# Retention and a gated feed-forward on one core: the first batch cast and transposed by pairs of heads, every second score tile in other banks

## The chip, the cores and the metric

The kernel runs on one core of a Trainium2 chip. A core has five engines that each work through their own queue in order: TensorE (PE, with PEld for its weight loads), VectorE (DVE), ScalarE (ACT), GpSimd (POOL) and SyncE (SP), which here only issues DMAs. ACT's queue issues DMAs too, the transposing ones. The metric is the time of one execution on the device, in microseconds; less is better.

## The reference

`B, H, S, D` are 8, 8, 576 and 64; the feed-forward goes from 512 to 2048 and back, over 4608 tokens.

```python
scores = scale * np.matmul(q, k.transpose(0, 1, 3, 2))
Dmat = np.where(rel >= 0, gamma[:, None, None] ** rel[None, :, :], 0.0)
attn = np.matmul(scores * Dmat[None], v)
x = attn.transpose(0, 2, 1, 3).reshape(B * S, H * D)
h = x @ w_in
out = (h * np.clip(h + 3.0, 0.0, 6.0) / 6.0) @ w_out
```

So each head's scores decay with distance and are causal; there is no softmax. The heads' outputs side by side are the rows of x, and those go through two matrix products with a hard swish between them.

## The kernel before

**Tiling.** Each batch has 576 positions: four chunks of 128, and a tail of 64. Two batches' tails are packed into one chunk, so there are 36 chunks. The decay is split into a factor on Q and factors on K and V, which the casts to fp16 multiply in; what is left of it within a chunk is a 0/1 mask (`mask01`, or `maskt` for a tail). Across chunks a running state, K transposed times V, carries the past.

**Steps.** The order of all work is written out in a string, `PROGRAM` (L35 to L79), and `act` (L628) carries out its words one after the other. Since each engine's queue is in order, the string sets for each engine what comes behind what. The words:

- `L i.h` (load0) loads half of the heads of Q (i = 0) or K (i = 1) of batch 0; `V t` loads a chunk of V of batch 0; `l n` (load) loads Q, K and V of chunk n; `W a.i` (wload) loads block i of w_in (a = 0) or w_out (a = 1), 512 KB each. All of these are issued on SP, in this order.
- `C` (cast0, L203) casts the first batch's Q or K by halves of the heads, `c n.i` (cast, L161) casts chunk n's Q, K or V, `w a.i` (wcast, L547) casts a weight block. The last letter is the engine: v for VectorE, g for GpSimd, s for ScalarE.
- `X` (xpose0, L218) transposes the first batch's Q or K on PE and copies it from PSUM to `wout16`, which stands in as its place until w_out is cast into it. `K` (kback, L232) transposes K back, for the state. `y n` (xpose_pe, L254) transposes chunk n on PE with a copy from PSUM; `x n` (xpose, L176) does it by a transposing DMA on ACT's queue.
- `s n` (ret1, L269) computes chunk n's scores into PSUM and masks them on DVE into `at` (L284); a number after it says how many warm matmuls, which compute nothing that is used, go ahead.
- `o n` (ret2, L292) multiplies the masked scores by V and adds what the state gives (L300, L306), updates the state (L325), copies the result on ACT to `xt` (L330) and casts the state on ACT to `s16` (L336), which the next chunk's `o` reads.
- `u` (up, L365) and `h` (up_half, L371) are pieces of the first product of the feed-forward: matmuls (L369, L385), a relu on ACT (L352), and on DVE the rest of the hard swish (L357).
- `p j` is a piece of the second product for batch 0, in the plain way (L412), with copies to `osb` after p7. For the other batches the second product is made of seven smaller ones, `P b.j` (product, L454), with sums of blocks built on DVE by `e b.j` (enc, L429) and `t j` (tbuild, L561).

**Banks.** PSUM has a tile "sc" of two banks (scores), "xp" and "st" of one each, and four buffers "mm" of one bank each, which X, K, h, u, p and P take in turn. The next user of a buffer waits until the one before has been read.

Of the kernel before, what the change touches and what calls it, by code (L numbers as in the profile page):

```python
# [10 lines left out]
FP32 = mybir.dt.float32  # L11
FP16 = mybir.dt.float16
ACTF = mybir.ActivationFunctionType
ALU = mybir.AluOpType
# [18 lines left out]


PROGRAM = """  # L35
H19 L0.0 L0.1 L1.0 L1.1 C0.0v C0.1v V0 W0.0 W0.1 V1 V2 V3 W0.2 W0.3 c0.2g
C1.0v X0.0s W0.7 X0.1s X1.0s C1.1v X1.1s s0.4 K0v w0.0s s1 c1.2g K1v o0
w0.1g s2.8 o1 s3 c2.2g w0.2g o2 h0.0.0.1 W0.4 c3.2g o3 W0.5 h0.0.2.3 w0.3v
W1.0 h0.1.0.1.8 W1.6 W0.6 W1.7 W1.1 W1.2 w0.5g h0.1.2.3 W1.3 l4 l5 W1.4 W1.5
u0.4 u0.5 u0.6 l6 w0.7g u0.7 w0.4g u0.8 w1.7s u0.9 l7 w0.6g w1.3g w1.6v  # L40
c4.0g u0.10 w1.0s u0.11 u0.12 u0.13 u0.14 u0.15 w1.1g c4.1v c5.0g p0 y4v l8
w1.2s p1 s4 p2 c5.1g y5v p3 w1.5s l9 c4.2g s5 w1.4g o4 t0 c5.2g p4 l10 l11
c6.0g c6.1g c6.2v c7.0v c7.1v c7.2g l12 c8.0g p5 y6s p6 l13 t1 c8.1g o5 s6
c9.0g c9.1g c8.2g p7 y7v h1.0.0.8 h1.0.1.9 s7 o6 h1.0.2.10 h1.0.3.11 l14
c9.2g l15 c10.0g c10.1g c11.0g c11.1g c10.2g x8 h1.0.4.12 h1.0.5.13 o7 x9
h1.0.6.14 h1.0.7.15 h1.1.0.8 h1.1.1.9 h1.1.2.10 h1.1.3.11 e1.1.0.4 h1.1.4.12
t2 h1.1.5.13 c11.2g l16 x10 l17 c12.0g c12.1g h1.1.6.14 c12.2g h1.1.7.15
e1.1.4.8 e1.2.0.8 s8 t3 P1.0 x11 P1.1 e1.3.0.8 P1.2 o8 c13.0g c13.1g c13.2g
s9 P1.3 x12 e1.4.0.8 P1.4 l18 o9 l19 c14.0g c14.1g c14.2g P1.5 P1.6 h2.0.0.8
h2.0.1.9 s10 x13 h2.0.2.10 h2.0.3.11 h2.0.4.12 o10 l20 s11 x14 c15.0g  # L50
h2.0.5.13 h2.0.6.14 o11 s12 c15.1g c15.2v h2.0.7.15 h2.1.0.8 h2.1.1.9 l21
s13 o12 h2.1.2.10 h2.1.3.11 x15 h2.1.4.12 c16.0g c16.1g c17.0g e2.1.0.4
c17.1g c16.2g l22 c17.2g h2.1.5.13 h2.1.6.14 x16 h2.1.7.15 o13 c18.0g
e2.1.4.8 e2.2.0.8 x17 P2.0 s14 c18.1g P2.1 e2.3.0.8 l23 P2.2 s15 o14 c19.0v
c19.1g c18.2g e2.4.0.8 x18 P2.3 s16 o15 l24 P2.4 x19 c19.2g P2.5 s17 o16
c20.2g P2.6 l25 u3.0 u3.8 s18 o17 u3.1 c20.0g c20.1g c21.0g c21.1g c21.2g
u3.9 x20 u3.2 u3.10 u3.3 l26 c22.2g c22.0g c22.1g u3.11 e3.3.0.4 u3.4 x21
e3.1.0.4 l27 u3.12 u3.5 u3.13 o18 c23.0g c23.1g s19 u3.6 u3.14 c23.2g u3.7
u3.15 e3.1.4.8 e3.2.0.8 P3.0 s20 o19 l28 c24.0g e3.4.0.8 P3.1 x22 P3.2
e3.3.4.8 c24.2g P3.3 s21 o20 x23 P3.4 c25.2g P3.5 c24.1g c25.0v c25.1g s22  # L60
P3.6 l29 l30 u4.0 u4.8 o21 u4.1 u4.9 c26.0g u4.2 x24 l31 c26.1g c26.2v l32
u4.10 u4.3 o22 c27.0g u4.11 u4.4 u4.12 e4.3.0.4 u4.5 u4.13 e4.1.0.4 x25 s23
u4.6 c27.1g c27.2g u4.14 u4.7 u4.15 e4.1.4.8 e4.2.0.8 l33 s24 o23 e4.3.4.8
c28.0g c28.1g x26 P4.0 c28.2g P4.1 P4.2 s25 e4.4.0.8 l34 o24 c29.0g c29.1g
c29.2g P4.3 x27 x28 l35 P4.4 P4.5 s26 o25 P4.6 u5.0 u5.8 u5.1 u5.9 s27 o26
u5.2 u5.10 u5.3 u5.11 e5.3.0.4 e5.1.0.4 x29 c30.2g c30.0g c30.1v u5.4 u5.12
u5.5 u5.13 s28 o27 u5.6 u5.14 u5.7 u5.15 x30 e5.1.4.8 e5.2.0.8 c31.2g c31.0g
c31.1g c32.2g c32.0g e5.4.0.8 P5.0 P5.1 c32.1g s29 o28 x31 c33.0g x32 c33.1v
P5.2 e5.3.4.8 P5.3 s30 o29 x33 P5.4 P5.5 P5.6 u6.0 u6.8 u6.1 c33.2v s31 u6.9
u6.2 o30 u6.10 u6.3 s32 o31 u6.11 u6.4 c34.0g c34.1g c35.0g x34 e6.1.0.4  # L70
u6.12 u6.5 o32 s33 u6.13 e6.3.0.4 u6.6 u6.14 u6.7 u6.15 e6.1.4.8 e6.2.0.8
s34 c35.1g c34.2g o33 e6.3.4.8 x35 P6.0 e6.4.0.8 P6.1 P6.2 P6.3 s35 o34
c35.2v P6.4 P6.5 o35 P6.6 u8.0 u8.8 u8.1 u8.9 u8.2 u8.10 u8.3 u8.11 u8.4
u8.12 u8.5 u8.13 u8.6 e8.1.0.4 u8.14 u8.7 u8.15 e8.1.4.8 e8.2.0.8 e8.3.0.4
P8.0 P8.1 e8.4.0.8 P8.2 P8.3 e8.3.4.8 P8.4 P8.5 P8.6 u7.0 u7.8 u7.1 u7.9
u7.2 u7.10 u7.3 u7.11 e7.1.0.4 u7.4 u7.12 u7.5 e7.3.0.4 u7.13 u7.6 u7.14
u7.7 u7.15 e7.1.4.8 e7.2.0.8 e7.3.4.8 e7.4.0.8 P7.0 P7.1 P7.2 P7.3 P7.4 P7.5
P7.6
"""  # L79
E_TAIL = 544  # L80

# [2 lines left out]
def kernel(  # L84
# [9 lines left out]
    nc = tc.nc  # L94
    B, H, S, D = q.shape
    NTOK, DM = out.shape
    DFF = moe_w_in.shape[1]
    P = 128
    HP = H // 2
# [87 lines left out]
    qk0 = {}  # L187
# [12 lines left out]
            qk0["st"][:, ix, hs, :, :].rearrange("p h r d -> p h (r d)"),  # L200
            src.rearrange("h (p r) d -> p h (r d)", r=4))

    def cast0(ix, hh, eng):  # L203
        hs = slice(4 * hh, 4 * hh + 4)
        tab = (tq if ix == 0 else tkv)[:, 5:9, hs].rearrange("p r h -> p h r")
        out = (qk0["16"][:, ix, :, :].rearrange("p r (h d) -> p h r d", h=H)
               [:, hs, :, :])
        eng.tensor_tensor(out=out, in0=qk0["st"][:, ix, hs, :, :],
                          in1=tab.unsqueeze(3).to_broadcast([P, 4, 4, D]),
                          op=ALU.mult)  # L210

    def copy(eng, dst, src):
        if eng == "v":
            nc.vector.tensor_copy(dst, src)
        else:
            nc.scalar.copy(dst, src)

    def xpose0(ix, hh, eng):  # L218
        tp = psum.tile([P, 2, 4, P], FP16, tag="mm", bufs=4, name="tp")
        for a in range(2):  # L220
            for r in range(4):
                n0 = (2 * hh + a) * P
                nc.tensor.transpose(tp[:, a, r, :],
                                    qk0["16"][:, ix, r, n0:n0 + P], ident)
        p0 = 4 * ix + 2 * hh
        dst = wout16[:, p0:p0 + 2, :].rearrange("z a (p r) -> z a p r", r=4)
        copy(eng, dst, tp.rearrange("z a r p -> z a p r"))
        if ix == 1 and hh == 1:
            for t in range(NC4):
                qkTs[(0, 0, t)] = wout16[:, 0:8, t * P:(t + 1) * P]  # L230

# [18 lines left out]
    def warm(ps, n, w=P):  # L250
        for _ in range(n):
            nc.tensor.matmul(ps, zero16[:, 0:P], zero16[:, 0:w], start=True, stop=True)
# [13 lines left out]
        else:  # L266
            nc.scalar.copy(qt, tp)

    def ret1(c, nwarm=0):  # L269
        kind, b, t = c  # L270
        qt = qkTs[c]
        sc = psum.tile([P, 2, HP, P], FP32, tag="sc", name="sc")
        if nwarm:
            warm(sc[:, 0, 0, :], nwarm)
        for p in range(HP):
            for z in range(2):
                nc.tensor.matmul(sc[:, z, p, :],  # L277
                                 qt[z * D:z * D + D, HP + p, :],
                                 qt[z * D:z * D + D, p, :],
                                 start=True, stop=True)  # L280
        at = work.tile([P, 2, HP, P], FP16, tag="at", bufs=2, name="at")
        ats[c] = at
        m = mask01 if kind == 0 else maskt
        nc.vector.tensor_tensor(  # L284
            out=at.rearrange("p z a i -> p (z a) i"),
            in0=sc.rearrange("p z a i -> p (z a) i"),
            in1=m[:, :].unsqueeze(1).to_broadcast([P, 2 * HP, P]),
            op=ALU.mult)

    state = [None]  # L290

# [284 lines left out]
    order = []  # L576
# [51 lines left out]
    def act(w):  # L628
        kind, n, e = w[0], [int(x) for x in w[1:].rstrip("svg").split(".")], w[-1]
        if kind == "H":  # L630
            xp = psum.tile([P, HP, P], FP32, tag="xp", name="xp")
            warm(xp.rearrange("p a n -> p (a n)"), n[0], BLK)
        elif kind == "L":
            load0(*n)
        elif kind == "C":
            cast0(*n, ENG[e])
        elif kind == "X":
            xpose0(*n, e)
        elif kind == "K":
# [66 lines left out]
```

## Time and profile before

| | |
|---|---|
| median of 5 runs | 305.73 us (304.67 to 307.56) |
| profiled execution | 304.67 us, of which the span of the engines' work is 302.5 us |
| PE | 290.5 us busy, 2887 matmuls |
| DVE, ACT, POOL | 237.6, 141.3, 109.5 us busy |
| DMA | 53.93 MB, 178 GB/s over the span |
| PE granted clock | full throughout |

A group's line in the profile has the source line, the engine, the operation, what it writes and reads, a count, and then the busy time. In an answer by time the first two numbers are start and duration in us, from the span's start; several neighbours of one kind are merged (x4), and what ended the engine's idle time before stands in brackets. A list of waits has engine and line, what ended the wait, the total in us, how often, and the longest. A busy PE is not PE at its peak: matmuls are pipelined and their ends modelled.

### The profile page before, as it was taken

How to read it: one execution, taken by the hardware profiler on the slowest of the kernel's cores; microseconds unless marked ns; L12 is line 12 of the kernel's file. 1: busy time of each engine (PE TensorE's matmuls, PEld its weight loads, DVE VectorE, ACT ScalarE, POOL GpSimd, SP SyncE). 2: the span in 40 equal slices, each digit the busy share in tenths (PEclk: the TensorE clock that was granted, in tenths of full speed). 3: DMA queues.
4: the chain of work that ended last, by engine and by line, in shares of the span. 5: the costliest groups of instructions: out<-in, count | busy, mean ns of one | idle time of the engine just before them, and what ended most of it. 6: DMA issues, size and time to landing. Idle time of an engine off the chain costs nothing.

```text
span 302.5 us, 7125 instructions
## 1 busy us (share of the span) xinstructions
PE 290.5 (96%) x2887; PEld 198.4 (66%) x2887; DVE 237.6 (79%) x335; ACT 141.3 (47%) x259; POOL 109.5 (36%) x120
## 2 busy tenths in 40 slices
PE   8669999998999999999999999999999999999995
PEld 2456445787788878547854786468556864684584
DVE  6567858779959898799778967998699767957963
ACT  2656804764237633574156425743386226405610
POOL 3164374868455535657176153334300000000000
PEclk9999999999999999999999999999999999999999
DMA  7999999999999999999999999999312130014004
GB/s 239 300 293 394 288 279 217 218 201 200 297 148 195 239 220 226 213 197 220 221 212 199 265 211 191 213 218 201 122 38 19 52 106 0 0 46 96 2 0 139
DMA packets 149728, 53.93 MB, mean 178 GB/s; under 512 B 134848, under 2 KB 145088, under 8 KB 149696
## 3 DMA queue, kind: packets, MB, share of 16 engines
q1 hardware_dynamic: 120128, 46.15, 71.0%
q10 hardware_dynamic: 29568, 7.34, 17.9%
q8 instruction: 22, 0.36, 0.6%
q14 instruction: 10, 0.08, 0.1%
HBM read 36.70 MB, written 9.44 MB: 153 GB/s over the span
## 4 chain that ended last, share of the span: by engine, by line
PE 88%; SPq 4%; DVE 3%; DMA 2%; POOL 1%; ACT 0%; issue 0%
PE ph L369 31%; PE accB L483 10%; PE ph L385 9%; PE accC L483 9%; PE accA L483 9%; PE accD L483 5%; PE po L412 5%; PE xp L300 4%; PE sc L277 3%; DMA wst<-in_moe_w_in_dram 2%; SPq L247 2%; PE xp L306 2%; SPq L539 1%; DVE g L357 1%; PE state L325 1%; DVE ss L447 1%
## 5 line engine op out<-in xcount | busy, mean ns | idle before, releaser
L357 DVE SCALAR_TENSOR_TENSOR g<-u,ph 128x512 f16<-128x512 f32 x144 | 95.6, 684 | 25.4 <-ACT u L352 24.2
L352 ACT ACTIVATE u<-ph 128x512 f32<-128x512 f32 x144 | 84.2, 597 | 66.1 <-PE ph L369 38.0
L369 PE MATMUL ph<-xt,win 128*128 128x512 f16 x368 | 82.5, 379 | 0.0
L369 PEld LDWEIGHTS <-win 128*128 128x128 f16 x432 | 41.4, 98 | 47.7 <-issue 0.3
L483 PEld LDWEIGHTS <-ss 128*128 128x128 f16 x512 | 48.8, 98 | 8.6 <-DVE ss L447 2.4
L172 POOL TENSOR_TENSOR v<-st,tkv 128x512 f16<-128x512 f32 x31 | 35.4, 1145 | 47.8 <-DMA st<-in_v_dram 32.8
L284 DVE TENSOR_TENSOR at<-sc,mask 128x1024 f16<-128x1024 f32 x32 | 39.0, 1219 | 7.7 <-PE sc L277 7.6
L172 POOL TENSOR_TENSOR qk<-st,tq 128x512 f16<-128x512 f32 x29 | 31.4, 1083 | 35.2 <-PE state L325 14.5
L483 PEld LDWEIGHTS <-g 128*128 128x128 f16 x384 | 36.9, 98 | 5.5
L172 POOL TENSOR_TENSOR qk<-st,tkv 128x512 f16<-128x512 f32 x28 | 32.4, 1159 | 8.4 <-DMA st<-in_k_dram 4.1
L385 PE MATMUL ph<-xt,win 128*128 128x256 f16 x288 | 33.3, 273 | 0.0
L330 ACT ACTIVATE xt<-xp 128x512 f16<-128x512 f32 x32 | 19.1, 597 | 28.1 <-PE xp L306 20.9
L483 PE MATMUL accB<-tmat,ss 128*128 128x256 f16 x256 | 30.7, 273 | 0.3 <-DVE ss L447 0.2
L483 PE MATMUL accA<-wout,g 128*128 128x256 f16 x256 | 30.6, 273 | 0.0
L385 PEld LDWEIGHTS <-win 128*128 128x128 f16 x288 | 27.4, 98 | 3.6
L447 DVE TENSOR_TENSOR ss<-g 128x1024 f16<-128x1024 f16 (+1 forms) x30 | 21.9, 732 | 0.3
L300 PE MATMUL xp<-at,v 128*64 128x128 f16 x288 | 19.9, 225 | 1.5 <-POOL v L172 1.5
L300 PEld LDWEIGHTS <-v 128*64 128x64 f16 x288 | 14.0, 109 | 8.1 <-issue 2.5
L336 ACT CAST s<-state 64x256 f16<-64x256 f32 x48 | 17.3, 361 | 0.5
L483 PE MATMUL accC<-tmat,ss 128*128 128x256 f16 x128 | 15.5, 273 | 1.0 <-DVE ss L447 1.0
L412 PE MATMUL po<-wout,g 128*128 128x512 f16 x64 | 15.3, 379 | 0.6 <-DVE g L357 0.6
L503 ACT COPY osb<-accA 128x512 f32<-128x512 f32 x8 | 4.7, 586 | 23.9 <-PE accA L483 23.9
(87 smaller groups left out, 264.5 us busy)
## 6 DMA issues: line engine op xcount, KB each, us to landing
st<-in_v_dram SPq DMA_DIRECT2D x32, 256.0 KB, 6.4
out_dram<-osb SPq DMA_DIRECT2D x32, 256.0 KB, 4.7
st<-in_q_dram SPq DMA_DIRECT2D x28, 256.0 KB, 6.1
st<-in_k_dram SPq DMA_DIRECT2D x28, 256.0 KB, 5.9
wst<-in_moe_w_in_dram SPq DMA_DIRECT2D x4, 512.0 KB, 6.8
tmat<-in_moe_w_in_dram SPq DMA_DIRECT2D x4, 512.0 KB, 9.1
wst<-in_moe_w_out_dram SPq DMA_DIRECT2D x4, 512.0 KB, 10.3
g<-in_moe_w_out_dram SPq DMA_DIRECT2D x4, 512.0 KB, 8.4
```

What stands on the lines that cost most here:

```text
L172: eng.tensor_tensor(out=dst, in0=st[:, ix, :, :], in1=tab.unsqueeze(2).to_broadcast([P, H, D]), op=ALU.mult)
L284: nc.vector.tensor_tensor(out=at.rearrange("p z a i -> p (z a) i"), in0=sc.rearrange("p z a i -> p (z a) i"), in1=m[:, :].unsqueeze(1).to_ ...
L300: nc.tensor.matmul(xp[rows[z], p, :], vt[:, 2 * p + z, :], at[:, z, p, :], start=(p == 0), stop=False, skip_group_check=True)
L330: nc.scalar.activation(xts[b][:, :, t * P:(t + 1) * P], xp, ACTF.Copy, scale=0.125)
L336: nc.scalar.copy(s16[rows[z], :, rows[z]], sp[rows[z], :, :])
L352: nc.scalar.activation(u, ph, ACTF.Relu, bias=0.5, scale=1.0 / 6.0)
L357: nc.vector.scalar_tensor_tensor(out=dst, in0=uv, scalar=1.0, in1=pv, op0=ALU.min, op1=ALU.mult)
L369: nc.tensor.matmul(ph, win16[:, m, P * fc:P * fc + P], xt[:, m, :], start=(m == 0), stop=(m == NCC - 1))
L385: nc.tensor.matmul(ph[:, 256 * j:256 * j + 256], win16[:, m, P * fc:P * fc + P], xt[:, m, cs], start=(m == 0 and j == 0), stop=(m == NCC - 1),
L412: nc.tensor.matmul(po, g[:, fc, P * mc:P * mc + P], wout16[:, fc, :], start=(fc == 0), stop=(fc == NFC - 1))
L447: nc.vector.tensor_tensor(out=dst, in0=a, in1=c, op=op)
L483: nc.tensor.matmul(ps[:, m, :], lhs(fc, m), rhs[:, fc, :], start=(first and fc == 0 and m == 0), stop=(fc == HF - 1 and m == 1), skip_grou ...
```

## The change

Casts and transposes of the first batch go by pairs of heads instead of by four heads, so there are eight of each instead of four, each half as wide, and `K0` goes from DVE to ACT. A word `S n` does what `s n` does, but puts the scores of each parity of heads into an "mm" buffer of its own instead of into "sc", and masks them in two instructions; chunks 1 and 3 use it. The string of the order is new as a whole: the first loads, casts and weight blocks come in another order and partly on other engines, and later words move by a few places (for example `s6` now follows `y6` with nothing of PE between, `t2` stands ahead of `e1.1.0.4`, `x16` behind `o13`). The loads are the same in number and size.

```diff
 PROGRAM = """
-H19 L0.0 L0.1 L1.0 L1.1 C0.0v C0.1v V0 W0.0 W0.1 V1 V2 V3 W0.2 W0.3 c0.2g
-C1.0v X0.0s W0.7 X0.1s X1.0s C1.1v X1.1s s0.4 K0v w0.0s s1 c1.2g K1v o0
-w0.1g s2.8 o1 s3 c2.2g w0.2g o2 h0.0.0.1 W0.4 c3.2g o3 W0.5 h0.0.2.3 w0.3v
-W1.0 h0.1.0.1.8 W1.6 W0.6 W1.7 W1.1 W1.2 w0.5g h0.1.2.3 W1.3 l4 l5 W1.4 W1.5
-u0.4 u0.5 u0.6 l6 w0.7g u0.7 w0.4g u0.8 w1.7s u0.9 l7 w0.6g w1.3g w1.6v
-c4.0g u0.10 w1.0s u0.11 u0.12 u0.13 u0.14 u0.15 w1.1g c4.1v c5.0g p0 y4v l8
-w1.2s p1 s4 p2 c5.1g y5v p3 w1.5s l9 c4.2g s5 w1.4g o4 t0 c5.2g p4 l10 l11
-c6.0g c6.1g c6.2v c7.0v c7.1v c7.2g l12 c8.0g p5 y6s p6 l13 t1 c8.1g o5 s6
-c9.0g c9.1g c8.2g p7 y7v h1.0.0.8 h1.0.1.9 s7 o6 h1.0.2.10 h1.0.3.11 l14
...
+L0.0 L0.1 C0.0v L1.0 C0.2v L1.1 C0.1v W0.0 W0.1 V0 V1 H19 V2 V3 W0.4 W0.2
+W0.3 X0.0s W0.5 C0.3g X0.1s C1.0v X0.2s X0.3s C1.1v X1.0s X1.1s C1.2v X1.2s
+C1.3v X1.3s s0.4 c0.2g c1.2g W0.6 S1 K0s w0.0s K1v w0.1g W0.7 o0 s2 o1 S3
+c2.2g o2 h0.0.0.1 w0.3s c3.2g o3 h0.0.2.3 h0.1.0.1.8 w0.2g W1.0 W1.6 W1.1
+W1.2 W1.3 w0.5g w0.6g l4 h0.1.2.3 l5 w0.7s W1.7 W1.4 w0.4g W1.5 u0.4 u0.5
+u0.6 l6 l7 l8 w1.1g w1.6v u0.7 w1.3g u0.8 u0.9 w1.0s u0.10 u0.11 u0.12 c4.0g
+u0.13 u0.14 u0.15 w1.2s c4.1g p0 w1.5s y4v c5.0g p1 c4.2g p2 w1.4g l9 w1.7s
+c5.2g c5.1v y5v s4 p3 c6.0g s5 o4 c6.1g c6.2v l10 p4 l11 p5 c7.0g c7.1v
+c8.0g c8.1g l12 c7.2g t0 t1 l13 c9.0g p6 y6s s6 o5 p7 y7s h1.0.0.8 c8.2g
+h1.0.1.9 o6 s7 c9.1g h1.0.2.10 h1.0.3.11 c9.2v c10.0g c10.2g c10.1g x8
...
-    def cast0(ix, hh, eng):
-        hs = slice(4 * hh, 4 * hh + 4)
+    def cast0(ix, p0, eng):
+        hs = slice(2 * p0, 2 * p0 + 2)
...
-    def xpose0(ix, hh, eng):
-        tp = psum.tile([P, 2, 4, P], FP16, tag="mm", bufs=4, name="tp")
-        for a in range(2):
-            for r in range(4):
-                n0 = (2 * hh + a) * P
-                nc.tensor.transpose(tp[:, a, r, :],
-                                    qk0["16"][:, ix, r, n0:n0 + P], ident)
-        p0 = 4 * ix + 2 * hh
-        dst = wout16[:, p0:p0 + 2, :].rearrange("z a (p r) -> z a p r", r=4)
-        copy(eng, dst, tp.rearrange("z a r p -> z a p r"))
-        if ix == 1 and hh == 1:
+    def xpose0(ix, p0, eng):
+        tp = psum.tile([P, 4, P], FP16, tag="mm", bufs=4, name="tp")
+        for r in range(4):
+            nc.tensor.transpose(tp[:, r, :],
+                                qk0["16"][:, ix, r, p0 * P:p0 * P + P], ident)
+        copy(eng, wout16[:, 4 * ix + p0, :].rearrange("z (p r) -> z p r", r=4),
+             tp.rearrange("z r p -> z p r"))
+        if ix == 1 and p0 == 3:
...
-    def ret1(c, nwarm=0):
+    def ret1(c, nwarm=0, two=False):
         kind, b, t = c
         qt = qkTs[c]
-        sc = psum.tile([P, 2, HP, P], FP32, tag="sc", name="sc")
+        if two:
+            sc = [psum.tile([P, HP, P], FP32, tag="mm", bufs=4, name="sc")
+                  for _ in range(2)]
+        else:
+            full = psum.tile([P, 2, HP, P], FP32, tag="sc", name="sc")
+            sc = [full[:, z, :, :] for z in range(2)]
...
-        nc.vector.tensor_tensor(
-            out=at.rearrange("p z a i -> p (z a) i"),
-            in0=sc.rearrange("p z a i -> p (z a) i"),
-            in1=m[:, :].unsqueeze(1).to_broadcast([P, 2 * HP, P]),
-            op=ALU.mult)
+        pieces = ([(at[:, z, :, :], sc[z], HP) for z in range(2)] if two else
+                  [(at.rearrange("p z a i -> p (z a) i"),
+                    full.rearrange("p z a i -> p (z a) i"), 2 * HP)])
+        for dst, src, n in pieces:
+            nc.vector.tensor_tensor(
+                out=dst, in0=src, op=ALU.mult,
+                in1=m[:, :].unsqueeze(1).to_broadcast([P, n, P]))
```

## The prediction

> **What bounds the kernel now.** I read the page's busy times first, then what TensorE (PE) waited for after 24 us, then the opening in order of time, engine by engine.
>
> ```profile
> PE 290.5 (96%) x2887; PEld 198.4 (66%) x2887; DVE 237.6 (79%) x335; ACT 141.3 (47%) x259; POOL 109.5 (36%) x120
> ```
>
> ```profile
> PE accC L483 <- DVE ss L447: 1.0, 1, 1.0
> PE po L412 <- DVE g L357: 0.6, 2, 0.4
> PE accB L483 <- DVE ss L447: 0.2, 1, 0.2
> ```
>
> The second fence is the whole list of PE's waits from 24 us to the end: 1.8 us. From there the kernel is PE's own work, and nobody removes any of that. So a reordering can gain what PE lacks before 24 us, plus at most 1.8 us, and it can lose whatever new wait it puts into the dense part. The opening decides when the dense part starts:
>
> ```profile
> 8.90 3.90 ACT L216 COPY wout<-tp 128x1024 f16<-128x1024 f16 x4 [6.34 <-PE tp L223]
> ...
> 17.24 1.22 DVE L284 TENSOR_TENSOR at<-sc,mask 128x1024 f16<-128x1024 f32 x1 [0.44 <-PE sc L277]
> ...
> 18.95 1.23 DVE L284 TENSOR_TENSOR at<-sc,mask 128x1024 f16<-128x1024 f32 x1 [0.49 <-PE sc L277]
> ...
> 20.16 1.04 POOL L559 CAST win<-wst 128x1024 f16<-128x1024 f32 x1 [2.14 <-DMA wst<-in_moe_w_in_dram]
> ...
> 21.16 1.04 POOL L172 TENSOR_TENSOR v<-st,tkv 128x512 f16<-128x512 f32 x1
> ...
> 22.25 0.25 PE L300 MATMUL xp<-at,v 128*64 128x128 f16 x2 [1.47 <-POOL v L172]
> ...
> 23.83 0.61 PE L252 MATMUL ph<-zero 128*128 128x128 f16 x8
> ...
> 25.92 3.00 POOL L559 CAST win<-tmat 128x1024 f16<-128x1024 f32 x3 [3.72 <-DMA tmat<-in_moe_w_in_dram]
> ```
>
> The masks stand 1.71 us apart although one takes 1.22: each waits about 0.45 for scores, which wait for the one "sc" tile. But the masks are not what ends last. o3 (L300 at 22.25) waits for the V cast at 21.16, which POOL holds behind weight cast w0.2, which waits for its DMA at 20.16. After o3 come its copy to xt (22.93 to 23.53), the half-up h0.0.2.3, the eight warm matmuls, and at 24.44 h0.1.0.1: the dense part.
>
> [...] landings follow issue order (V0 by 11.11, V1 15.00, W0.2 20.16, W0.5 25.9, W0.6 29.96), and the engines' mean share is about 1 throughout, so a load's landing is set by what is queued ahead. [...]
>
> **The change, part by part.**
>
> *Casts and transposes by pairs.* Four DVE casts of 1.23 us become seven of 512 elements on DVE (0.68 each, the row of L172) and one on POOL (1.04, while it idles from 4.3 to 11.1). The last, C1.3, ends at 9.85 + 2 x 0.65 = 11.15, as before (9.85 + 1.23). PE's 19 warm matmuls still end at 8.4, so the earlier Q casts gain nothing. ACT's copies: [...] the trace has 0.535 for paired relus. They can start 0.25 earlier, after four transposes: 8.65 + 8 x 0.53 = 12.9 against 12.80. The last scores then need only one pair: first mask at about 13.3 against 13.25. Net 0.
>
> *S1 and S3 in "mm" banks.* S1's scores no longer wait for mask 0. DVE then does mask 0 (13.3 to 14.5), S1's two halves (0.69 each, together 1.3, to 15.8), K1's copy (16.5), mask 2 (17.7), and mask 3 once S3 is there. PE runs in order, and o1 ahead of S3 needs s16 of o0. ACT now does K0's copy (14.1 to 15.1), w0.0 (to 16.1), then o0's xt (0.6) and s16 casts (0.74): 17.35 against 17.10. o1 ends at 18.1, S3 18.5, mask 3 at 18.55 to 19.85 against 20.18. Gain 0.3, not on the path: o3 also needs s16 of o2, at 20.8 (before 20.96).
>
> *c3.2g ahead of w0.2g.* V3 has the same bytes before it as before (four half loads, two weight blocks, V0 to V2), so it lands between V2 (by 17.0) and W0.2 (20.16), about 18.3; its cast ends about 19.4. POOL no longer holds o3, which is bound by s16: 20.85 against 22.25. This is the gain, 1.4 us.
>
> *The new load order takes it back.* V0 now stands behind W0.0 and W0.1: it lands about 13.7 instead of 11.1, cast 14.75, just ahead of need. W0.4 is put ahead of W0.2 and W0.3. W0.3 is now third after V3, the old place of W0.7. From 20.16 (W0.2) to 25.9 (W0.5) four blocks landed, 1.435 each, so that place lands at 20.16 + 2 x 1.435 = 23.0. And w0.3 is now cast on ACT **between the relu of h0.0.0.1 and o3's copy to xt**. Queued behind it: xt, the relu of h0.0.2.3, then everything. ACT is free at 21.5, waits to 23.0, casts to 24.0 (1.05), copies xt to 24.6. PE has done o3, h0.0.2.3 and the warm matmuls by 23.1 and waits. h0.1.0.1 at 24.6 against 24.44: **+0.15**. The landing is uncertain by 0.7 either way, so -0.55 to +0.85; never before 23.1, where PE arrives. w0.2 (lands 21.6, POOL to 22.7) is in time for u0.4.
>
> *w0.7 on ACT, ahead of u0.4's relu.* W0.7 moves three places on from W0.3's: 23.0 + 3 x 1.435 = 27.3, cast to 28.35. The relus of u0.4 to u0.6 wait, and u0.8 needs u0.4's bank: relu 28.95, L357 0.69 later, 29.65; PE comes there at 26.35 + 3.5 = 29.85. Hidden, with 0.2 to spare; a W0.7 later than 27.5 costs PE what it is late. W0.5, W0.6 (24.5, 25.9) and w0.4 (POOL, by 28.0) are in time.
>
> *W1 blocks.* l4 and l5 land one block earlier (W1.7 goes behind them), W1.4 and W1.5 after the same bytes (43.4, 45.74). ACT does w1.5 and w1.7 in a row, to 47.8; p5 (48.5), p7 and o4's copy bear that. C6.2 and c7.1 go ahead of t0 on DVE; K of chunk 7 lands at 51.17, so t0 and t1 (2.31 + 1.29) end at 55.4, mask 6 at 56.6, p7's second output copy about 57.25; PE needs the mask at 58.5 and that bank at 57.6. Hidden, thinly.
>
> *s6 straight after y6.* Before, p6 lay between:
>
> ```profile
> 50.03 0.61 PE L263 MATMUL tp<-ident,qk 128*128 128x128 f16 x8
> 50.48 1.89 PE L412 MATMUL po<-wout,g 128*128 128x512 f16 x8
> ```
>
> ```profile
> 50.68 1.01 ACT L267 COPY qkT<-tp 128x1024 f16<-128x1024 f16 x1 [2.75 <-PE tp L263]
> ```
>
> The transposes are done at 50.64, the copy at 51.69, and p6 covered it. Now PE goes y6, s6, with o5 and p7 queued behind s6: it waits for the copy, 1.05 plus some 0.03 to start: **+1.08**. Nothing later repays it.
>
> *The rest of the order.* y7's copy on ACT has two half-ups and o6 before s7. t2 ahead of e1.1.0.4 shifts DVE's backlog within one queue: P1.0 waits then instead of P1.1, and e1.2.0.8 ends where it did (76.93): the 1.2 us of stall stay. Five more POOL casts go to DVE (0.68 each); spacings between each s and its o, and each sum and its product, stay above what DVE needs (mask 1.22, sum 1.22). x16, now behind o13's copies on ACT, would issue about 107.1, take the 7.2 that transposes there took, and land at 114.3 for s16 at 114.56. Bounds: 0 to +1, below nothing by the 1.2 us stall if DVE got ahead. I take +0.1.
>
> Sum: 0.15 + 1.08 + 0.1 = +1.3. The profiled execution took 304.67 (span 302.5 and 2.2 around it), so 306.0; the median of the runs shown is 1.06 above it, so 307.0.
>
> **The rivals.** *Early W0.3 (0.16).* If W0.3 lands by 21.5, ACT isn't held: the dense part starts at 23.2 (-1.2), and +1.08 for s6 cancels it: 305.7. For it: blocks late in the opening move at 390 GB/s; against: 190 to 250 GB/s from 14 to 18 us, with V's 256-byte pieces. *Gain kept whole (0.08).* W0.3 early, and y6's copy hidden because something else binds PE there: -1.2, 304.5. *ACT behind late weights (0.21), the one that ends slower.* ACT takes w0.3 and w0.7 ahead of the copies that free PE. If blocks land 0.9 later than I count, h0.1.0.1 slips to 25.5 (+1.05) and w0.7 ends at 29.25, so the relus back up through four banks (+0.7 at u0.8, and up to 0.4 at w1.5), then s6 +1.08 and x16 +0.5: +3.7, 309.4. It decides from 0.6 late on. *The masks do pay* is no case of its own: mask 3's 0.3 us ends before s16.
>
> **How the numbers follow.** The likeliest case, +0.4 to +2.3, has 0.55: 306.1 to 308.0, taken at 307.0. To it the range adds the early-W0.3 case and most of the slow one: 304.8 to 309.6. About 1% (3.1 us) is what a measurement here can tell from no change. Below 302.7 only the whole gain with a stall removed: 0.03. Above 308.8 the slow rival: 0.21. Within: 0.76.
>
> **What would show it.** On PE a wait of about 1.1 at L277 for ACT's L267 near 52 us. ACT idle near 21.5 to 23, released by the DMA of w_in, at L557. o3 (L300) near 20.9. DVE masks of 1.22, 0.69, 0.69. PE's waits after 24 us near 3 us instead of 1.8. I am wrong if W0.3's cast starts much off 23.0, if PE doesn't wait at s6, or if a wait over 1 us shows at x or e after 60 us.

## The result, and the profile after

The changed kernel takes 307.70 us in the median (305.31 to 311.29), the kernel before, run beside it, 306.26 (304.56 to 308.24). The ratio is 1.0046, with a 95% interval of 1.0033 to 1.0059: +1.4 us (+1.0 to +1.8), where +1.3 was forecast. So the total was right. Several of the terms that made it up were not, as will be seen.

The profiled execution took 308.12 us, its span is 306.0 (302.5 before). The difference of the two traces is larger than that of the medians: the profiled execution of before lies 1.6 under its median, that of after 0.4 over.

First the waits of PE from 24 us on, the list that had 1.8 us before. It now has 5.7:

```profile
PE ph L389 <- ACT xt L334: 2.5, 1, 2.5
PE accA L487 <- DVE g L361: 1.6, 1, 1.6
PE sc L279 <- ACT qkT L264: 1.1, 1, 1.1
PE po L416 <- DVE g L361: 0.5, 1, 0.5
```

The first lies in the opening. Its lines in order of time:

```profile
12.65 2.42 DVE L290 TENSOR_TENSOR at<-sc,mask 128x1024 f16<-128x1024 f32 x3 [1.73 <-PE sc L279]
...
15.97 1.22 DVE L290 TENSOR_TENSOR at<-sc,mask 128x1024 f16<-128x1024 f32 x1 [0.31 <-PE sc L279]
...
17.09 2.04 POOL L172 TENSOR_TENSOR v<-st,tkv 128x512 f16<-128x512 f32 x2
...
17.88 1.29 DVE L290 TENSOR_TENSOR at<-sc,mask 128x512 f16<-128x512 f32 x2 [0.68 <-PE sc L279]
...
20.33 0.25 PE L304 MATMUL xp<-at,v 128*64 128x128 f16 x2
...
23.68 1.04 ACT L561 CAST win<-wst 128x1024 f16<-128x1024 f32 x1 [2.49 <-DMA wst<-in_moe_w_in_dram]
24.63 0.59 ACT L334 ACTIVATE xt<-xp 128x512 f16<-128x512 f32 x1
...
25.28 3.06 PE L389 MATMUL ph<-xt,win 128*128 128x256 f16 x16 [2.53 <-ACT xt L334]
```

Masks 0 and 1 do follow one another (one stretch of three pieces, 2.42 us). The V of chunks 2 and 3 is cast back to back, and o3 starts at 20.33 instead of 22.25: 1.9 us won. Then ACT stands for 2.49 us in front of the cast w0.3, whose DMA it awaits, with o3's copy to `xt` queued behind it, and PE stands for 2.53 us. The dense part starts at 25.28. In the trace of before, its first matmuls stand at 24.28:

```profile
24.28 1.91 PE L385 MATMUL ph<-xt,win 128*128 128x256 f16 x16
```

(The prediction's 24.44 is where the profile lets the warm matmuls ahead of them end, 23.83 + 0.61. Compared by starts, the dense part comes 1.00 later.)

The 16 matmuls at 25.28 have something else: they take 3.06 us, where those of before take 1.91. By windows (the last three columns are PE's granted clock, the DMA share and GB/s):

```profile
20.00:25.00 5.00, 2.75 (x44) 2.12 (x43) 1.44 (x3) 2.46 (x5) 1.04 (x1) 1.00 1.03 392
25.00:30.00 5.00, 4.72 (x23) 2.88 (x23) 2.06 (x3) 2.94 (x6) 3.06 (x3) 0.66 1.05 385
```

After the hole the granted clock is 0.66 over five microseconds; by windows of one microsecond it is 0.5 from 26 to 29. From the start of h0.1.0.1 to p0, the first piece of the second product, it is 39.05 - 25.28 = 13.77 us, against 36.52 - 24.28 = 12.24 before. So in this execution the opening lost 1.00 up to the start of the dense part and 1.53 behind it, 2.53 together. It is compared with one trace at full clock; four traces with nearly the opening of before, in which the clock was lower for a while, reach p0 at 37.2 to 37.7 (table below).

Then s6, 55 us in:

```profile
54.29 0.61 PE L260 MATMUL tp<-ident,qk 128*128 128x128 f16 x8
54.94 1.01 ACT L264 COPY qkT<-tp 128x1024 f16<-128x1024 f16 x1 [4.61 <-PE tp L260]
56.01 0.40 PE L279 MATMUL sc<-qkT 64*128 64x128 f16 x8 [1.10 <-ACT qkT L264]
```

It is the wait that was forecast, 1.10 for 1.08. And last the product P1.0, which waits 1.56 us for DVE's swish at 77.17. DVE's queue before it, then POOL's:

```profile
73.05 2.86 DVE L576 TENSOR_TENSOR tmat<-wout 128x1024 f16<-128x1024 f16 x2
75.84 0.68 DVE L451 TENSOR_TENSOR ss<-g 128x1024 f16<-128x1024 f16 x1
76.44 2.47 DVE L361 SCALAR_TENSOR_TENSOR g<-u,ph 128x512 f16<-128x512 f32 x4
```

```profile
72.88 1.04 POOL L172 TENSOR_TENSOR qk<-st,tkv 128x512 f16<-128x512 f32 x1 [1.17 <-DMA st<-in_k_dram]
74.02 1.35 POOL L172 TENSOR_TENSOR v<-st,tkv 128x512 f16<-128x512 f32 x1
```

The line of 2.86 us is t2, two operations on fp16 in SBUF. They take that long here, beside two casts of POOL. Below they take 1.29.

### The profile page after: what moved, and what is told of

Read it like the earlier page. It is cut to its first block, busy times and chain, and to the rows that moved or that the text cites. A ratio compares the mean times of both kernels' runs of the same rounds, so it can differ in the third digit from the quotient of the medians.

```text
span 306.0 us, 7129 instructions
## 1 busy us (share of the span) xinstructions
PE 291.3 (95%) x2879; PEld 199.3 (65%) x2879; DVE 241.7 (79%) x341; ACT 146.0 (48%) x267; POOL 104.0 (34%) x116
## 4 chain that ended last, share of the span: by engine, by line
PE 87%; SPq 5%; DVE 3%; DMA 3%; ACT 1%; issue 0%
PE ph L373 31%; PE accB L487 9%; PE ph L389 9%; PE accA L487 9%; PE accC L487 9%; PE accD L487 5%; PE po L416 4%; PE xp L304 4%; PE sc L279 3%; SPq L244 3%; DMA wst<-in_moe_w_in_dram 3%; PE xp L310 2%; DVE g L361 1%; PE state L329 1%; DVE tmat L576 1%; SPq L543 1%
## 5 line engine op out<-in xcount | busy, mean ns | idle before, releaser
L373 PEld LDWEIGHTS <-win 128*128 128x128 f16 x432 | 41.7, 98 | 48.2 <-issue 0.8
L172 POOL TENSOR_TENSOR qk<-st,tq 128x512 f16<-128x512 f32 x29 | 30.7, 1058 | 55.5 <-DMA st<-in_q_dram 17.8
L172 POOL TENSOR_TENSOR v<-st,tkv 128x512 f16<-128x512 f32 x29 | 32.8, 1136 | 31.1 <-DMA st<-in_v_dram 13.2
L290 DVE TENSOR_TENSOR at<-sc,mask 128x1024 f16<-128x1024 f32 (+1 forms) x34 | 39.0, 1155 | 5.4 <-PE sc L279 5.3
L389 PE MATMUL ph<-xt,win 128*128 128x256 f16 x288 | 34.3, 278 | 2.5 <-ACT xt L334 2.5
L172 POOL TENSOR_TENSOR qk<-st,tkv 128x512 f16<-128x512 f32 x26 | 29.5, 1135 | 10.1 <-PE sc L279 6.2
L389 PEld LDWEIGHTS <-win 128*128 128x128 f16 x288 | 28.1, 100 | 6.7 <-issue 2.6
L451 DVE TENSOR_TENSOR ss<-g 128x1024 f16<-128x1024 f16 (+1 forms) x30 | 22.9, 775 | 0.3
L487 PE MATMUL accC<-wout,ss 128*128 128x256 f16 x128 | 15.3, 273 | 0.0
```

Of the source, the lines that this page charges most:

```text
L172: eng.tensor_tensor(out=dst, in0=st[:, ix, :, :], in1=tab.unsqueeze(2).to_broadcast([P, H, D]), op=ALU.mult)
L290: nc.vector.tensor_tensor(out=dst, in0=src, op=ALU.mult, in1=m[:, :].unsqueeze(1).to_broadcast([P, n, P]))
L373: nc.tensor.matmul(ph, win16[:, m, P * fc:P * fc + P], xt[:, m, :], start=(m == 0), stop=(m == NCC - 1))
L389: nc.tensor.matmul(ph[:, 256 * j:256 * j + 256], win16[:, m, P * fc:P * fc + P], xt[:, m, cs], start=(m == 0 and j == 0), stop=(m == NCC - 1),
L451: nc.vector.tensor_tensor(out=dst, in0=a, in1=c, op=op)
L487: nc.tensor.matmul(ps[:, m, :], lhs(fc, m), rhs[:, fc, :], start=(first and fc == 0 and m == 0), stop=(fc == HF - 1 and m == 1), skip_grou ...
```

## The experiments

All are timed against the kernel before. A ratio is turned into microseconds with 306.26; a difference of two ratios takes their intervals as independent. "The rest" is what follows p0. The mean granted clock of each whole execution is known too. Half clock for 3.4 us, called a low stretch here, takes 0.0056 off it (in the trace of the changed kernel the clock is at half from 25.84 to 29.26 us, and the mean is 0.994), so the number of low stretches can be read from it.

The theory to test: the change loses in two places of its order, at W0.3 (ACT held, then the low clock) and at s6, and nothing else in it matters. The rivals: another part costs as well (the masks, the pairs, the rest of the order), or a wait that is taken away only gives its time to another.

**p6 back between y6 and s6.**

```diff
-c8.1g l12 c7.2g t0 t1 l13 c9.0g p6 y6s s6 o5
+c8.1g l12 c7.2g t0 t1 l13 c9.0g y6s p6 s6 o5
```

(The minus line is the changed kernel, as in the following three.)

> The changed kernel with p6 again between y6 and s6. Theory: the wait of 1.1 us at s6 goes and nothing takes its place, so 1.0 to 1.1 us less than the changed kernel, that is about +0.35 us (+-0.4) against before. Rival: TensorE then waits at P1.0 or P1.2 for VectorE instead (its waits there grow from 1.6 to 2.6 us) and nothing is gained.

Ratio 1.0007 [0.9986, 1.0028]: 1.2 us (+-0.75) less than the changed kernel. PE's waits from 24 us:

```profile
PE ph L389 <- ACT xt L334: 3.0, 1, 3.0
PE po L416 <- DVE g L361: 0.5, 1, 0.5
```

s6's wait is gone. So is P1.0's, which the edit doesn't touch. DVE's queue there:

```profile
73.19 1.29 DVE L576 TENSOR_TENSOR tmat<-wout 128x1024 f16<-128x1024 f16 x2
```

t2 is alone here: POOL's next cast waits for its DMA until 75.10. So this trace gives 1.1 to s6 and 1.56 to t2, 2.7 in all, and the median no more than about 2. What of the 1.2 is s6's own can't be read from this run.

**40 more warm matmuls before h0.1.0.1.** They fill the hole and shorten no wait.

```diff
-c2.2g o2 h0.0.0.1 w0.3s c3.2g o3 h0.0.2.3 h0.1.0.1.8 w0.2g
+c2.2g o2 h0.0.0.1 w0.3s c3.2g o3 h0.0.2.3 h0.1.0.1.48 w0.2g
```

> The changed kernel with 48 warm matmuls instead of 8 ahead of h0.1.0.1, so that TensorE has work while it waits for xt. If the idle 2.5 us is what lowers the granted clock after it (0.66 from 25 to 30 us in the profile of the changed kernel), the clock stays at 1.0, h0.1.0.1 and h0.1.2.3 take 1.75 us instead of 3.06, and the time falls by up to 1.3 us to about +0.1 us against before. If the low clock is an accident of that one execution, the time is that of the changed kernel, +1.4 us.

Ratio 0.9992 [0.9970, 1.0013], 1.65 us (+-0.8) under the changed kernel. In its trace the clock is full from 18 us on, and the 48 matmuls of u take 10.52 us instead of 11.09. Work that computes nothing buys time here. But in this trace h0.1.0.1 starts at 26.50, later than in the changed kernel, and p0 comes only 0.44 earlier. That the low clock behind the hole is what the 1.65 us were lost to isn't shown, and the mean clocks speak against it. Executions of the changed kernel take 307.1 us on average with no low stretch (3 of them) and 307.4 with one (25); with the 48 matmuls it is 305.6 (7) and 306.3 (5). At the same clock, 1.1 to 1.5 of the 1.65 are still there. Over all kernels timed here but the one at 1.0112 below, each compared with itself, a low stretch goes with 0.5 us (+-0.2) more: an estimate, a straight line through the times and clocks of 241 executions. And t2 again happens to take 1.29 in this trace, so the median may have a part of that too.

**W0.4 behind W0.2 and W0.3.**

```diff
-W0.0 W0.1 V0 V1 H19 V2 V3 W0.4 W0.2 W0.3 X0.0s W0.5
+W0.0 W0.1 V0 V1 H19 V2 V3 W0.2 W0.3 W0.4 X0.0s W0.5
```

> The changed kernel with W0.4 issued behind W0.2 and W0.3 instead of ahead of them. Theory: W0.3 lands one block (about 1.4 us) earlier, ACT casts it about 22.3 instead of 23.7, h0.1.0.1 starts about 23.9 instead of 25.3, TensorE idles some 1.1 us there, so 1.3 us less than the changed kernel, and up to 1.3 more if the clock now stays up: -1.2 to +0.1 us against before. Rival: other blocks (W0.7) become the wait in the up-projection and nothing is gained (+1.4 us).

Ratio 0.9987 [0.9960, 1.0013], 1.8 us (+-0.9) under the changed kernel. One place less in the queue moves w0.3's cast from 23.68 to 21.71, PE's wait shrinks to 0.56, and the clock stays full throughout:

```profile
21.71 1.04 ACT L561 CAST win<-wst 128x1024 f16<-128x1024 f32 x1 [0.52 <-DMA wst<-in_moe_w_in_dram]
...
23.31 1.91 PE L389 MATMUL ph<-xt,win 128*128 128x256 f16 x16 [0.56 <-ACT xt L334]
```

The same 16 matmuls take 1.91 us at full clock, 1.15 less than the 3.06. But PE comes so early now that w0.7 is in the way: its block lands for a cast at 27.42, the relus of the pieces of u stand behind it on ACT, and PE waits for a buffer at u0.8:

```profile
27.42 1.04 ACT L561 CAST win<-tmat 128x1024 f16<-128x1024 f32 x1 [1.57 <-DMA tmat<-in_moe_w_in_dram]
...
29.73 7.07 PE L373 MATMUL ph<-xt,win 128*128 128x512 f16 x32 [1.07 <-DVE g L361]
```

That is what the rival expected, though it takes only a part of the gain.

**w0.3 behind o3's copies on ACT, w0.7 behind u0.7.**

```diff
-c2.2g o2 h0.0.0.1 w0.3s c3.2g o3 h0.0.2.3 h0.1.0.1.8 w0.2g
+c2.2g o2 h0.0.0.1 c3.2g o3 w0.3s h0.0.2.3 h0.1.0.1.8 w0.2g
...
-h0.1.2.3 l5 w0.7s W1.7 W1.4 w0.4g W1.5 u0.4 u0.5
-u0.6 l6 l7 l8 w1.1g w1.6v u0.7 w1.3g
+h0.1.2.3 l5 W1.7 W1.4 w0.4g W1.5 u0.4 u0.5
+u0.6 l6 l7 l8 w1.1g w1.6v u0.7 w0.7s w1.3g
```

> The changed kernel with the two weight casts on ACT put behind the copies that free TensorE: w0.3 behind o3, w0.7 behind u0.7. Loads unchanged. Theory: o3's copy no longer waits for W0.3, h0.1.0.1 starts about 23.2 instead of 25.3 with no idle time, u0.4 about 25 to 26 when w0.3 is cast; 1.5 to 3 us less than the changed kernel, that is -1.5 to 0 us against before. Rival: the weights' landing itself is the bound and TensorE waits at u0.4 or u0.8 instead (+1.4 us, the wait moved).

Ratio 0.9982 [0.9960, 1.0003], 2.0 us (+-0.8) under the changed kernel. h0.1.0.1 starts at 23.68, without idle time. A part of the gain goes to other waits, though:

```profile
PE accA L487 <- DVE g L361: 1.7, 1, 1.7
PE ph L373 <- DVE g L361: 1.3, 1, 1.3
PE sc L279 <- ACT qkT L264: 1.1, 1, 1.1
PE po L416 <- DVE g L361: 0.5, 1, 0.5
```

The 1.3 is for a swish that stands on DVE behind the cast w1.6, whose DMA DVE awaits for 1.95 us.

Three ways of mending the same place each give 1.65 to 2.0 us. That this place costs time is shown. How much of it is PE's wait and how much is what follows isn't, since the run that leaves the wait gains about as much.

**The casts later and p6 between.** The two edits above together.

> The changed kernel with the casts w0.3 and w0.7 later on ACT and p6 between y6 and s6, the load order left as changed. If the two add up: -2.0 - 1.2 = -3.2 us against the changed kernel, ratio about 0.994 to 0.997 against the kernel before. If W0.4 ahead of W0.3 still costs something of its own with the casts later, it is slower than the version with all three repairs by 0.5 us or more; otherwise the two are equal within 0.5.

Ratio 1.0001 [0.9979, 1.0023]. They don't add up: 0.994 to 0.997 was expected. Putting p6 between gives nothing on top of the later casts (+0.6, +-0.95). Its trace has no wait at s6, but P1.0 waits 1.2, t2 takes 2.48, and the clock is at half from 12 to 25 us.

**All three repairs.**

> The changed kernel with the three repairs together: W0.4 loaded behind W0.3, the casts w0.3 and w0.7 moved on ACT behind o3's copies and behind u0.7, and p6 back between y6 and s6. If the losses lie in these places and are separate (ACT held by W0.3, with the low clock that follows, and the wait of s6), the repairs add up: alone they gave -1.8 (load order), -2.0 (casts later) and -1.2 us (p6) against the changed kernel, the first two for the same wait, so together -2.8 to -3.2 against it, a ratio of 0.995 to 0.9965 against the kernel before, and no wait of 1.1 at s6. If removing one wait only hands the time to the next (the accA wait on the swish grows, as it did with the casts later), the ratio stays at 0.998 or above.

Ratio 0.9999 [0.9977, 1.0021]: nor do three. PE's waits, with p6 back in its place:

```profile
PE accA L487 <- DVE g L361: 1.7, 1, 1.7
PE ph L389 <- ACT xt L334: 1.2, 1, 1.2
PE po L416 <- DVE g L361: 0.5, 1, 0.5
PE xp L304 <- DVE at L290: 0.5, 1, 0.5
```

The second and the fourth are new, at 100 to 102 us. The rival is right about the sum: put together, the repairs bring the changed kernel down to the kernel before and not beneath it.

**s6 after y6 in the kernel before.** Here the minus line is the kernel before.

```diff
-c8.0g p5 y6s p6 l13 t1 c8.1g o5 s6
+c8.0g p5 p6 y6s s6 l13 t1 c8.1g o5
```

> The kernel before with p6 ahead of y6 and s6 straight after y6 (before o5). Theory: a wait of 1.1 us at s6 for the copy of y6, +1.0 to +1.1 us against before. Rival: covered by a wait that is there anyway (0).

Ratio 1.0003 [0.9982, 1.0024]: +0.1 us (-0.55 to +0.75), where +1.05 was expected. The trace has the wait all the same, and less of the next ones (1.2 for accC and accB before, 0.6 here):

```profile
PE sc L276 <- ACT qkT L266: 1.1, 1, 1.1
...
PE accB L482 <- DVE ss L446: 0.4, 2, 0.2
...
PE accC L482 <- DVE ss L446: 0.2, 1, 0.2
```

In the kernel before, t2 takes 2.38; here it takes 1.53. PE came to P1 later, and DVE lost less in t2. So "nothing later repays it" was wrong: by the medians most of it is repaid, and the trace shows 0.6 of that, 20 us on. Where the remainder is repaid stays open; in this trace a new wait of 0.3 for `qkT` takes some of it away again.

**c3.2g ahead of w0.2g in the kernel before.**

```diff
-o1 s3 c2.2g w0.2g o2 h0.0.0.1 W0.4 c3.2g o3
+o1 s3 c2.2g c3.2g w0.2g o2 h0.0.0.1 W0.4 o3
```

> The kernel before with the cast of V of chunk 3 ahead of w0.2 on GpSimd, nothing else. Theory: o3 is then bound by the state copy at about 21.0 instead of the cast at 22.2, and u0.4 starts 1.2 us earlier; w0.4 on GpSimd (28.96) then binds u0.8, which leaves 0.5 to 1.2 us of gain (-1.2 to -0.5 us against before). Rival: no gain (0), since the cast order moves the wait to the weights.

Ratio 1.0007 [0.9986, 1.0027], no gain. V is there in time, as predicted, and o3 is late all the same:

```profile
17.26 2.04 POOL L171 TENSOR_TENSOR v<-st,tkv 128x512 f16<-128x512 f32 x2
...
22.81 0.74 ACT L335 CAST s<-state 64x256 f16<-64x256 f32 x2
23.31 0.25 PE L299 MATMUL xp<-at,v 128*64 128x128 f16 x2
```

```profile
11.00:16.00 5.00, 3.65 (x36) 2.67 (x36) 2.29 (x3) 2.69 (x3) 1.77 (x2) 0.50 1.11 262
16.00:21.00 5.00, 4.89 (x75) 4.16 (x72) 3.10 (x4) 1.81 (x5) 3.79 (x5) 0.50 0.96 298
```

o3 waits for o2's `s16` (L335), and the chain to it is slow because PE ran at half clock from 11 to 21 us (eight score matmuls take 0.61 us there, and 0.40 at full clock in the trace of before). The clock, granted over the whole execution, was 0.983 to 0.989 in all executions of this kernel that the ratio takes. So none of them had the full clock at which the 1.4 us were read. At a lower clock the wait for V that the edit takes away is small in the first place. In the trace of the experiment before this one, with the loads and casts of before and half clock from 12 to 20 us, o3 waits 0.16 for V instead of 1.47:

```profile
22.76 0.25 PE L299 MATMUL xp<-at,v 128*64 128x128 f16 x2 [0.16 <-POOL v L171]
```

With the opening of before under the changed rest (below), at half clock from 13 to 20 us, PE shows no wait for it. With a single low stretch (the next run) it is 1.60. So the 1.4 us can be had where the clock is full for most of the time up to o3, and the kernel before seldom has that: in the last set of its runs 59 of 66 executions have two low stretches or more.

**Only S1 and S3, in the kernel before.** `ret1` is that of the change. These are two of the 36 score tiles; the change, too, leaves the others in "sc".

```diff
-X0.1s X1.0s C1.1v X1.1s s0.4 K0v w0.0s s1 c1.2g K1v o0
-w0.1g s2.8 o1 s3 c2.2g w0.2g o2
+X0.1s X1.0s C1.1v X1.1s s0.4 K0v w0.0s S1 c1.2g K1v o0
+w0.1g s2.8 o1 S3 c2.2g w0.2g o2
```

> The kernel before with only the scores of chunks 1 and 3 in two mm buffers each and masked in two instructions. Theory: the masks follow one another more closely, but the V cast of chunk 3 and the state copies hold o1 to o3, so 0 (+-0.3 us) against before. Rival: the single score tile was on the path, -0.5 us or more.

Ratio 1.0026 [1.0003, 1.0049], +0.8 us (+0.1 to +1.5). The masks come closer, and o3 waits for V as before (1.60 us):

```profile
18.21 2.46 DVE L292 TENSOR_TENSOR at<-sc,mask 128x1024 f16<-128x1024 f32 x3 [0.53 <-PE sc L281]
...
22.40 1.04 POOL L171 TENSOR_TENSOR v<-st,tkv 128x512 f16<-128x512 f32 x1
```

That masks following one another gain nothing is shown. Why they should cost 0.8 isn't: the trace reaches p0 at 37.63, within the 37.16 to 37.64 of two other traces that have the kernel before's opening, and its waits after that are 1.8, as before. It stays open.

**Only the pairs, in the kernel before.** `cast0` and `xpose0` are those of the change; the eighth cast is on DVE here, on POOL in the change.

```diff
-H19 L0.0 L0.1 L1.0 L1.1 C0.0v C0.1v V0
+H19 L0.0 L0.1 L1.0 L1.1 C0.0v C0.1v C0.2v C0.3v V0
...
-C1.0v X0.0s W0.7 X0.1s X1.0s C1.1v X1.1s s0.4
+C1.0v C1.1v X0.0s W0.7 X0.1s X0.2s X0.3s X1.0s X1.1s C1.2v C1.3v X1.2s
+X1.3s s0.4
```

> The kernel before with the first batch's casts and transposes by pairs of heads alone, the loads in the order of before. The prediction's step says net 0: -0.3 to +0.3 us, first mask within 0.3 us of before's. If the eight narrower copies cost ACT more than their cadence of 0.53 suggests, the first mask comes 0.5 to 1 us later and o3, bound by the V cast on GpSimd, hides it: then too about 0, but with a later mask 0.

Ratio 1.0018 [0.9992, 1.0044], +0.55 us (-0.25 to +1.35), which doesn't tell a loss from none. ACT's eight copies run from 8.46 to 12.47, 0.50 us each, where the four of before took 3.90 together. The first mask starts at 12.87; PE then waits 2.7 for the V cast of chunk 3 (1.5 before).

**The changed opening, the kernel before's rest.**

```diff
 l4 h0.1.2.3 l5 w0.7s W1.7 W1.4 w0.4g W1.5 u0.4 u0.5
-u0.6 l6 l7 l8 w1.1g w1.6v u0.7 w1.3g u0.8 u0.9
+u0.6 l6 u0.7 u0.8 u0.9 l7 w1.3g w1.6v c4.0g u0.10
...
```

(The minus line is the changed kernel; w1.7 goes behind w1.5.)

> The changed kernel's words up to u0.4, then the order of before (without the casts already done; w1.7 behind w1.5, because its load comes later). If the loss is s6 behind y6 alone, this is as fast as before (0 +- 0.4 us). If the opening itself costs (ACT held by w0.3 until 23.7, TensorE idle for 2.5 us before h0.1.0.1, then its clock lower for some us), this is +0.8 to +2.2 us against before. If the later order is what costs, it is level with before or better.

Ratio 1.0112 [1.0063, 1.0161], but for a reason of its own:

```profile
134.03 2.06 ACT L356 ACTIVATE u<-ph 128x512 f32<-128x512 f32 x4 [5.16 <-POOL qk L172]
...
135.40 1.86 PE L373 MATMUL ph<-xt,win 128*128 128x512 f16 x4 [3.71 <-DVE g L361]
```

ACT's queue stands for 5.16 us at a transposing DMA whose input POOL hasn't cast yet, the relus behind it come late, and PE waits 3.7 at 135 us. The four matmuls right behind it take 1.86 us, where four of that shape take 1.03 at full clock (L412 at 42.63, before): by the end of the wait the clock is down. In the page's slice from 131.6 to 139.4 us its mean is 0.7 to 0.8, which would be half clock for 3.1 to 4.6 us. The two orders don't fit together there. The run says nothing on the opening. It shows what an `x` can cost that is issued ahead of its cast.

**The kernel before's opening, the changed rest, p6 between.** The other way round; the minus line is the kernel before:

```diff
 h0.1.0.1.8 W1.6 W0.6 W1.7 W1.1 W1.2 w0.5g h0.1.2.3 W1.3 l4 l5 W1.4 W1.5 u0.4
-u0.5 u0.6 l6 w0.7g u0.7 w0.4g u0.8 w1.7s u0.9
+u0.5 u0.6 l6 w0.7g w0.4g w0.6g l7 l8 w1.1g w1.6v u0.7 w1.3g u0.8 u0.9
...
```

> The kernel before's opening, up to the first piece of the feed-forward, with the changed kernel's order behind it, except that p6 stands between y6 and s6. It tests the term 'rest of the order' (taken as +0.1). If that holds: 0 to +0.3 us against the kernel before, with P1.0 waiting 1.2 or so for DVE in place of the 1.2 of accC. If the rest of the order costs by itself (t2 ahead of the sums beside a GpSimd cast, x16 late): +0.5 to +1.5.

Ratio 0.9972 [0.9950, 0.9993]: 0.9 us (0.2 to 1.5) **faster than the kernel before**, the lowest ratio of all. It differs from the first experiment in the opening alone, and from the kernel before in the rest. P1.0 waits 1.4 in place of accC's and accB's 1.2. That splits the change by medians: the rest of the order -0.9, the opening +1.1 (+-0.9, from 0.9972 to 1.0007), p6 away from between +1.2 (+-0.75, from 1.0007 to 1.0046). It is a split along one path, by runs of different sets. Since the repairs don't add up, another path would share the sum out otherwise. And the theory fails in its last part: something else in the order does matter, to the good.

**All traces in one table.** p0 is the start of the first piece of the second product; the rest runs from there to the span's end.

| kernel | p0 | rest | PE's waits in it | rest less waits | t2 |
|---|---|---|---|---|---|
| before | 36.5 | 266.0 | 1.8 | 264.2 | 2.38 |
| s6 after y6 | 37.2 | 267.2 | 2.6 | 264.6 | 1.53 |
| c3.2g ahead | 37.7 | 266.6 | 2.1 | 264.5 | 2.38 |
| only S1 and S3 | 37.6 | 266.2 | 1.8 | 264.4 | 1.53 |
| only the pairs | 38.8 | 265.5 | 1.2 | 264.3 | 1.53 |
| changed opening, rest of before | 37.4 | 272.3 | 6.0 | 266.3 | 2.51 |
| changed | 39.1 | 266.9 | 3.2 | 263.7 | 2.86 |
| p6 between | 40.4 | 264.4 | 0.5 | 263.9 | 1.29 |
| 48 warm matmuls | 38.6 | 266.0 | 1.8 | 264.2 | 1.29 |
| W0.4 behind | 36.6 | 266.2 | 2.4 | 263.8 | 1.29 |
| casts later | 37.2 | 267.0 | 3.3 | 263.7 | 2.13 |
| casts later, p6 between | 38.5 | 265.5 | 1.7 | 263.8 | 2.48 |
| all three | 37.5 | 267.8 | 3.9 | 263.9 | 2.13 |
| opening of before, changed rest, p6 between | 37.6 | 265.6 | 1.9 | 263.7 | 2.72 |

Once the few waits are taken off, the rest is about 264 us in every order, so the waits are nearly the whole account of it. (The one at 266.3 has its low clock at 135 us: by one low stretch, half of 3.4, some 1.7 more, an estimate. The changed orders are shorter than the others by some 0.5 that no wait explains.)

In the changed orders PE waits 0.8 to 1.7 us at P1.0, but for two: p6 between, and the 48 warm matmuls. The wait is what DVE loses just before; in the trace of the changed kernel that is beside POOL's casts at 72.88 and 74.02. Add what t2 takes beyond 1.29 and what the sum behind it (L451, 0.69 alone) takes beyond 0.69. In the order of the table that gives 1.57, 0, 0, 0.84, 1.68, 1.19, 1.67 and 1.43 for the eight changed orders, and PE waits 1.56, 0, 0, 0.84, 1.68, 1.18, 1.68 and 1.42. With W0.4 behind, for example, t2 is alone and the sum is not:

```profile
71.84 1.53 DVE L451 TENSOR_TENSOR ss<-g 128x1024 f16<-128x1024 f16 x1
```

In the changed kernel K of chunk 12 has landed for a cast at 72.88, and t2 starts at 73.05; with p6 between that cast waits for its DMA until 75.10, when t2 (73.19) and the sum (74.39) are done. Which of the two happens goes with no edit in particular: the changed kernel (p0 at 39.1) opens between the two that don't wait (40.4 and 38.6), and waits. Three of the four changed orders that open before 38 us lose 1.4 to 1.7 there, so a gain in the opening can be lost again at P1.0. One trace each doesn't show how often it happens.

## Why the prediction was right in size, and where it was not

- **Pairs, net 0.** Not contradicted (+0.55, -0.25 to +1.35). ACT's copies came 0.50 us apart, for the 0.53 it was reckoned with.
- **Masks, 0.3 off the path.** Right that they don't decide: o3 waits for V or for `s16`. The part alone came out at +0.8, unexplained.
- **c3.2g, the gain of 1.4.** In the trace of the changed kernel o3 starts at 20.33, even before the step's 20.85. Alone it brought nothing. The step read one trace in which the clock was full from end to end, and in the last set of runs of the kernel before only 3 of 66 executions had that; the median clock there is 0.988. At such a clock the wait for V was 0.16 or none in two traces, and the chain through `s16` bound o3.
- **W0.3 on ACT, +0.15.** This is the term that failed. The mechanism was as told, wait and queue included, but the landing was reckoned at 23.0 and the cast started at 23.68 (24.75 and 24.98 in the runs with 48 warm matmuls and with p6 between, which have the same load order). The pace between blocks was right, 1.33 us from w0.2's cast to w0.3's for 1.435: w0.2's cast, which waits for its block too, starts at 22.35 for the 21.6 foretold, so the queue as a whole was late. h0.1.0.1 came at 25.28 for 24.6. By starts it is 1.00 later than before, not 0.15, of which 0.16 is the prediction's reading of 24.44 for 24.28. What came behind it, 1.53 in that execution, was not in the reckoning. By medians the opening costs +1.1 (+-0.9).
- **w0.7 on ACT, hidden.** No wait shows at u0.8, but by luck: the cast starts at 28.86, past the step's own limit of 27.5, and only PE's lateness hides it. With W0.4 behind PE is in time, and a cast at 27.42 costs 1.07 there.
- **s6, +1.08.** The wait is 1.10, at the place foretold. Its price in time depends on what follows: 1.2 in the changed kernel, 0.1 in the kernel before, none on top of the later casts. That it is always repaid or never repaid isn't shown.
- **The rest of the order, +0.1.** Measured -0.9 (-1.5 to -0.2). That P1.0 would wait instead of P1.1 is right. That the stall is a constant 1.2 is not: it is 0 to 1.7, what t2 and the sum behind it take beyond their time alone. Where the 0.9 comes from isn't settled; in the traces the new rest, less its waits, is shorter by some 0.5.
- **x16, 0 to +1.** No wait shows there in the changed kernel.

So +0.15 + 1.08 + 0.1 became +1.1 + 1.2 - 0.9: the opening was undersized by as much as the rest was oversized. That they cancel, and that the sum of +1.3 was met, is luck; what is right for its reasons is the wait of W0.3 on ACT and that of s6. PE's waits after 24 us are 5.7 and not near 3, as two of them came out larger than told. The rival of ACT behind late weights was closer for the opening: W0.3 was late by 0.7, over its point of 0.6, and h0.1.0.1 came at 25.28 for its 25.5. Its further steps, relus backing up and a late x16, didn't come in the changed kernel, and so not its 309.4. Early W0.3 is what the load order with W0.4 behind makes of it, and that is worth 1.8 us: its ratio, 0.9987 (0.9960 to 1.0013), has room for the level with before that this rival foretold.

## What to carry to other kernels

A cast that waits for a DMA holds all that stands behind it in its engine's queue (2.49 us on ACT in the changed kernel): reckon the landing with its scatter (here 23.7 to 25.0 us in three traces with the same load order) and put the copies that PE needs ahead of it. A wait that PE shows in one place is not its price: add up the waits of the whole trace before and after, since the next one, here a DVE backlog, often gives or takes the same amount. And compare the clock of the one profiled execution with that of the others before taking its times for typical.

## What was not expected of the hardware

**The clock goes to half in steps.** In twelve of the fourteen traces PE's granted clock drops to 0.5 for about 3.4 us, or a multiple of it, somewhere between 10 and 31 us (3.4, 6.8, 10.2 or 13.6 us in all, by windows of one microsecond). In those of the kernel before and of W0.4 behind it doesn't. Over whole executions most mean clocks lie close to 1.0, 0.994, 0.989 and 0.983: steps of some 0.0056, which of 303 us is 1.7, half of 3.4. Some of it goes with idle time. After 21 us PE waits 2.5 us or more in four places: 2.53 in the changed kernel, 2.98 with p6 between, 2.68 with only the pairs, 3.71 at 135 us with the rest of before. Each time, and by the page's slices nowhere else until the last 10 us, half clock begins: at 135 us by the end of the wait, in the other three 0.6 to 1.2 us after its end (at 25.84, 27.74 and 23.76). No wait of 1.7 or less is followed by it. With the hole of the changed kernel filled by 48 matmuls it stays away. What starts the low stretches ahead of 21 us, and why one lasts 3.4, isn't shown.

The mean clock of the changed kernel (0.992) is no lower than that of the kernel before (0.988), so the number of low stretches doesn't explain the difference. In four of the five traces with nearly the opening of before they begin at 11 to 14 us and are over by 22. That isn't free either: p0 is then at 37.2 to 37.7, for 36.5 at full clock.

**VectorE beside GpSimd.** An fp16 product of 128x1024 in SBUF takes 0.68 us alone (two in 1.29). Beside casts of GpSimd it takes 1.42 and 1.53 in the changed kernel (two in 2.86), and the second cast there takes 1.35 instead of 1.04. In eight traces what t2 and the sum behind it take beyond their time alone is PE's wait at P1.0 to 0.01 us (above). Elsewhere it is the cast that takes longer: in the trace of before the sum at 69.46 keeps its 0.69, and the cast that starts beside it at 69.48 takes 1.58. Why the two lengthen one another isn't shown.
